# V in three column tiles with its third part behind the scores, one-bank turns of K and Q, and the attention weights turned in the forward pass

## The chip, the cores and the metric

The kernel runs on one core of a Trainium2 chip. The metric is the time of one execution on the device in microseconds (us), the median of several runs. The engines are PE (TensorE; PEld are its weight loads), DVE (VectorE), ACT (ScalarE), POOL (GpSimd) and SP (SyncE, which here only issues DMAs).

## The reference

The reference computes a block's output and the gradients of eleven of its inputs, all in bf16 (2048 tokens, width 512). The block is an adaLN-modulated recurrent memory attention followed by a gated GLU:

```python
def _A_ref(x, mem0, Wq, Wk, Wv, Wo, seg_len):        # seg_len 32, M = 8, H = 32 heads of 128
    mem = mem0
    for s in range(n_seg):                            # 64 segments, one after the other
        h = concat([mem, xs], axis=1)                 # 8 + 32 tokens
        q, k, v = h @ Wq, h @ Wk, h @ Wv              # per head
        p = softmax(where(mask, q k^T * scale, -1e9))
        o = (p v) @ Wo
        mem = o[:, :M]                                # the next segment's memory
        outs.append(o[:, M:])

def _fwd_reference(...):
    sa, ca, ga, sb, cb, gb = silu(c) @ w_mod
    x = x + ga * _A_ref(layernorm(x) * (1 + ca) + sa, ...)
    h = layernorm(x) * (1 + cb) + sb
    return x + gb * ((sigmoid(h @ w_gate) * (h @ w_up)) @ w_down)

out, vjp = jax.vjp(_fwd_reference, ...); grads = vjp(grad_out)
```

## The kernel before

`phase2` is the forward attention, `phase3` the GLU with its gradients and then the GLU's weight gradients, `phase4` the attention backwards, `phase5` the attention's weight gradients and the last layernorm. Instructions of the forward loop are pinned in the order in which the program writes them, on every engine and on SP (`self.pin(i0)`), so the order of the text is the order of work.

A segment has 40 tokens: 8 of memory and 32 of its own. The first 32 of them (memory and 24 tokens) depend on the segment before; the last 8 of four neighbouring segments do not, and are projected together for the group ("the tails", `b_pieces`, `proj_b`, 32 rows for the next group of four). `s4` is the place of a segment in its group.

`col_pass` is one pass of a projection: for each of four slices of the width, four matmuls of 512 columns that stand side by side in four column tiles of 32 rows. A pass covers 16 heads; tile j < 3 takes every third head of the first 24, tile 3 takes the heads 24 to 31. K, Q and V have two passes each. The result is copied to `RA[x]` (128 rows; `RAs` hold two of K and Q and one of V).

For K and Q the rows are turned by `turns` (eight transposes each into two half-filled PSUM banks) and copied into `XT[x]` by `to_heads`: "own" copies for tiles 0 to 2, "far" copies for tile 3. The first half of each goes by ACT, the second by DVE. For V, POOL copies 96 rows of `RA["v"]` into `Vst`, and `vshift` moves tile 3's heads to their rows by three small matmuls (into `sh_ps`) and one DVE copy. `v_tails` brings the tail rows of V into `Vst` by six DMAs on POOL's queue.

Then come the scores and their exponentials in three parts (`st_exp`), the denominators (`den`), the products with V (`pv`), the reciprocal and the scaling into `Ost` (part 1 on ACT, parts 0 and 2 on DVE), the turn of `Ost` into `OT` (`ott`), the product with Wo (`outproj`, into `at_ps`), its split in two bf16 halves (`split_pair`: `at_hi` on ACT, `at_lo` on DVE) and the fold (`sum_pair`, into `at_ft`). ACT copies `at_ft` into the memory columns of the next segment's `hT`, and with that the next segment's K can begin. Tail work fills PE ahead of the fold (`fill(s4, "f1")`) and behind it (`fill(s4, "f2")`): one pass of V, K and Q each at s4 = 0, 1, 2, and at s4 = 3 two chunks of 16 matmuls of the output projection of tails (`tail.chunk`). PSUM has five banks for all of these in turn (`psp`), and three for the scores.

SP's queue in a segment holds, in order: the stores of `VTr` and `Pst` of the segment before (the latter when POOL has scaled it), the row stores of K and Q (`rows_out`), two transposing DMAs (`VTr` from `Vst`, `Pst` from `ET`), and the stores of `Ost` (`OSR`) and `OT`. The tails' rows go in between.

Behind the GLU's pipeline, `phase3` computes the GLU's weight gradients (`wd_chunk` and the loop that follows it): 11 products of 512 columns and 32 of 448 columns, 16 matmuls each, whose rows are loaded by ACT's queue into a ring of two buffers. Between them `emit_setup` spreads 32 pieces from `p4_weights_setup_pieces`: each loads four heads of Wo, Wv, Wk or Wq (512 KB) into one of three staging slots, turns them by 16 transposes in four groups (into `wtp`), and DVE and ACT copy them to `WoT`, `WvT`, `WkT`, `WqT`, which `phase4` uses.

At the start, `load_heads` loads 24 heads of each of Wk, Wq, Wv in place and 8 to a staging place, from which three DVE copies put them in the order that tile 3 needs.

Of the kernel before, what the change touches and what calls it, by code (L numbers as in the profile page):

```python
# [40 lines left out]
class K:  # L41
# [43 lines left out]
    def alloc_dram(self):  # L85
# [26 lines left out]
        self.DHB = d("DHB", [NS // 4, 32, cfg.D], BF16)  # L112

# [323 lines left out]
    def phase2(self):  # L437
# [13 lines left out]
        with ExitStack() as ctx:  # L451
# [33 lines left out]
            RAs = [{x: ptiles(f"RA{i}" + x, 1, w=9 * 128)[0] for x in ("vkq", "kq")[i]} for i in range(2)]  # L485
            RAs[1]["v"] = RAs[0]["v"]
            RB = {x: ptiles("RB" + x, 1, w=9 * 128)[0] for x in "kq"}
            RBv = ptiles("RBv", 2, w=9 * 128)
# [17 lines left out]
            mem0 = pt.tile([M, D], BF16, name="mem0")  # L506
            with tc.tile_pool(name="p0", bufs=1) as p0:
# [14 lines left out]
                nc.sync.dma_start(mem0[:], io["A_mem0"].rearrange("o m d -> (o m) d"))  # L522
# [12 lines left out]
                place["v"] = self.load_heads(stage(2), Wv, io["A_Wv"])  # L535
# [70 lines left out]
            def b_pieces(t):  # L606

                bt = btails[t] = {}
                RBt = dict(RB, v=RBv[t % 2])

                def proj_b(x, hf):
                    hb = hxs[t][1]
                    pass_half(x, hf, lambda c: hb[:, c, :, :].rearrange("p s q -> p (s q)"), RBt[x], ("dve", "act")[hf])
                    if hf == 1 and x != "v":
                        rows_out(RBt[x], DR[x], t * nseg_t, nseg_t)

                def turn_b(x):
                    bt[x] = btp.tile([128, 8, 128], BF16, name="b_cols" + x)
                    tp = psp.tile([128, 8, 128], BF16, name="turn_ps", tag="p")
                    for i in range(8):  # L620
                        nc.tensor.transpose(tp[:, i, :], RBt[x][:, i * 128:(i + 1) * 128], self.ident[:, :])

                    def f():
                        for hf in range(2):
                            self.evac(("act", "dve")[hf], bt[x][:, 4 * hf:4 * hf + 4, :], tp[:, 4 * hf:4 * hf + 4, :])

                    evacs.append(f)

                P = lambda x, hf: (lambda: proj_b(x, hf))
                T_ = lambda x: (lambda: turn_b(x))  # L630
                d = {(s4, "f%d" % (hf + 1)): [P(x, hf)] for s4, x in enumerate("vkq") for hf in range(2)}
                d.update({(s4 + 1, "turn"): [T_(x)] for s4, x in enumerate("vkq") if x != "v"})
                return d
# [3 lines left out]
            def evac_turned():  # L637
                while evacs:
# [3 lines left out]
            firsts = {x: [f for k in ((s4, "f1"), (s4, "f2"), (s4 + 1, "turn")) for f in first.get(k, [])] + [evac_turned]  # L642
                      for s4, x in enumerate("vkq")}
            slots = {}

# [4 lines left out]
            norms = []  # L650
            mod_r = []
# [7 lines left out]
            tail = TailRows(self, sb2, psp, psp, 1, "ao", rows_b, 2, ptag="p")  # L659
# [14 lines left out]
            def v_tails(s):  # L674

                Vst, rb, o = Vsts[s % 2], RBv[(s // nseg_t) % 2], 8 * (s % nseg_t)
                for j in range(3):
                    nc.gpsimd.dma_start(Vst[96 + 8 * j:104 + 8 * j, 0:1024], rb[32 * j + o:32 * j + o + 8, 0:1024])
                    nc.gpsimd.dma_start(Vst[96 + 8 * j:104 + 8 * j, 1024:1408], rb[96 + o:104 + o, 384 * j:384 * j + 384])
# [9 lines left out]
            for s in range(NS):  # L689
# [11 lines left out]
                def proj(x, hf, eng):  # L701
                    pass_half(x, hf, lambda c: hT[:, c, :], RA[x], eng)
                    if hf == 1 and x != "v" and s < NS - 1:
# [6 lines left out]
                def turns():  # L710
                    tps = []
                    for x in "kq":
                        for hf in range(2):
                            tps.append((x, hf, ("act", "dve")[hf], turn_half(RA[x], hf)))
                            to_heads(tps[-1][2], XT[x], tps[-1][3][:], 4 * hf, 4, 32, 0, far=False)
                    for x, hf, eng, tp in tps:
                        to_heads(eng, XT[x], tp[:], 4 * hf, 4, 32, 0, own=False)
# [26 lines left out]

                def vshift():
                    sh = ps_f32("sh_ps")
                    shf = sh[:].rearrange("p g x -> p (g x)")
                    for hl in range(3):
                        nc.tensor.matmul(shf[32 * hl:32 * hl + 32, 0:384], lhsT=self.ident[96:128, 96:128],
                                         rhs=RA["v"][96:128, 384 * hl:384 * hl + 384], start=True, stop=True,  # L750
                                         tile_position=(96, 32 * hl))
                    nc.vector.tensor_copy(Vst[0:96, 1024:1408], shf[0:96, 0:384])
# [49 lines left out]
                if s == 0:  # L802
# [3 lines left out]
                    place["v"]()  # L806
                    load_wo(2)
                    for k in (1, 2, 3):
                        p1(1, k)
                    for f in firsts["v"]:  # L810
                        f()
                    v_tails(0)
                proj("v", 0, "dve")
                nc.gpsimd.tensor_copy(Vst[0:96, 0:512], RA["v"][0:96, 0:512])
                turns()
                proj("v", 1, "dve")
                nc.gpsimd.tensor_copy(Vst[0:96, 512:1024], RA["v"][0:96, 512:1024])
                if s == 0:
                    p1(1, 4)
                    p1(P1_AHEAD, 0)  # L820
                if s + 1 < NS:
                    v_tails(s + 1)
# [7 lines left out]
                vshift()  # L830
                st_exp(2)
                if s < NS - 1:
# [48 lines left out]
                self.pop_later()  # L881
                nc.sync.dma_start(self.OSR[s], gl3(Ost))
# [17 lines left out]
                fill(s4, "f2")  # L900
                if s4 == 3:
                    tail.chunk()
                tail.split()
# [53 lines left out]
    def phase3(self):  # L957
# [300 lines left out]
        with ExitStack() as ctx:  # L1258
            op_ = ctx.enter_context(tc.tile_pool(name="p3g_o", bufs=2, reuse_waits="tile"))
            psG = ctx.enter_context(tc.tile_pool(name="p3g_ps", bufs=4, space=PSUM, reuse_waits="tile"))  # L1260
            setup_pieces = self.p4_weights_setup_pieces(ctx)
# [80 lines left out]
    def p4_weights_setup_pieces(self, ctx):  # L1342
        nc, tc, cfg, io = self.nc, self.tc, self.cfg, self.io
        D, DC, H, E = cfg.D, cfg.DC, cfg.H, cfg.E
        HB = 4
        stg = ctx.enter_context(tc.tile_pool(name="p4stage", bufs=1, reuse_waits="tile"))
        sps = ctx.enter_context(tc.tile_pool(name="p4sps", bufs=2, space=PSUM, reuse_waits="tile"))
        pieces = []
        kk = [0]
        slots = [stg.tile([128, DC * HB * E], BF16, name=f"stage{i}") for i in range(2)]  # L1350
        slots = [t[:, :] for t in slots] + [self.flat(self.Wv, 2 * cfg.NT * 448, DC * HB * E)]
        np_ = [0]

        def slot(pat, **kw):
            np_[0] += 1
            return slots[np_[0] % 3].rearrange(pat, **kw)

        def qkv_piece(src_ap, dst, h0):
            def f():
                srcv = src_ap.rearrange("(c p) h e -> p c h e", p=128)  # L1360
                wn = slot("p (c h e) -> p c h e", c=DC, e=E)
                nc.sync.dma_start(wn, srcv[:, :, h0:h0 + HB, :])
                for hi in range(HB):
                    h = h0 + hi
                    tp = sps.tile([128, DC, 128], BF16, name="wtp")
                    for c in range(DC):
                        nc.tensor.transpose(tp[:, c, :], wn[:, c, hi, :], self.ident[:])
                    self.evac("dve" if kk[0] % 3 != 2 else "act", dst[:, h, :], tp[:, :, :].rearrange("p c d -> p (c d)"))
                    kk[0] += 1
            return f  # L1370

        def wo_piece(h0):
            def f():
                wov = io["A_Wo"].rearrange("h e d -> e h d")
                won = slot("p (h d) -> p h d", h=HB)
                nc.sync.dma_start(won, wov[:, h0:h0 + HB, :])
                for c in range(DC):
                    tp = sps.tile([128, HB, 128], BF16, name="wtp")
                    for i in range(HB):
                        nc.tensor.transpose(tp[:, i, :], won[:, i, c * 128:(c + 1) * 128], self.ident[:])  # L1380
                    self.evac("dve" if kk[0] % 3 != 2 else "act", self.WoT[:, c, h0 * E:(h0 + HB) * E],
                              tp[:, :, :].rearrange("p i e -> p (i e)"))
                    kk[0] += 1
            return f

        for h0 in range(0, H, HB):
            pieces.append(wo_piece(h0))
        for (src_ap, dst) in ((io["A_Wv"], self.WvT), (io["A_Wk"], self.WkT), (io["A_Wq"], self.WqT)):
            for h0 in range(0, H, HB):
                pieces.append(qkv_piece(src_ap, dst, h0))  # L1390
        return pieces

    def p4_weights_setup_transposes(self):
        with ExitStack() as ctx:
            for f in self.p4_weights_setup_pieces(ctx):
                f()

    def phase4(self):
# [3 lines left out]
        if not hasattr(self, "p4_ctx"):  # L1402
            self.p4_ctx = ExitStack()
            self.p4_weights_setup_begin()
            self.p4_weights_setup_transposes()
# [758 lines left out]
```

## Time and profile before

| | us |
|---|---|
| median of 3 runs | 3081.47 (3080.04 to 3082.02) |
| the profiled execution | 3080.64 |
| its span | 3078.9 |
| forward attention, first to last K pass | 18.9 to 977.4 |
| GLU weight gradients, until the attention backwards begins | 1346.0 to 1522.9 |
| mean granted clock of TensorE | 0.991 |

| stretch (us) | PE busy | DVE busy | ACT busy | POOL busy | DMA share |
|---|---|---|---|---|---|
| 100 to 500 | 395.84 | 239.62 | 211.69 | 278.73 | 0.80 |
| 500 to 1200 | 673.34 | 458.86 | 344.94 | 392.21 | 0.85 |

The profile is of one execution. A row of its order of time gives the start, the duration, the engine, the line, the operation, its output and inputs, the shape and the count; in square brackets stands the idle time of the engine ahead of it and what ended that. Matmuls overlap, so that what one adds to the path is the distance to the next start rather than its duration. The segments start about every 14.7 us.

### The profile page before, as it was taken

Reading aid. Unit: us, or ns where it says so; the run is one execution under the profiler, and the core shown is the slowest. Engines: PE = TensorE matmul, PEld = TensorE weight load, DVE = VectorE, ACT = ScalarE, POOL = GpSimd, SP = SyncE. Lnnn points to the kernel's source line nnn. Section 1 sums busy time; section 2 is a strip of 40 time slices with the busy share of each in tenths; the row PEclk is TensorE's granted clock in tenths of the full one; section 3 lists DMA queues with packets and bytes.
Section 4 is the critical chain, followed back from the end, with each engine's and each line's share of the span. In section 5 each row is a group of like instructions: output and inputs, shape, how many; then the busy total and the mean of one; then the engine's idle time right before and its main releaser. Section 6 shows DMA issues by size and latency. Waiting matters only on the chain.

```text
span 3078.9 us, 106050 instructions
## 1 busy us (share of the span) xinstructions
PE 2985.9 (97%) x43769; PEld 1821.5 (59%) x43845; DVE 1613.0 (52%) x3799; ACT 1254.4 (41%) x3056; POOL 1386.1 (45%) x2960
## 2 busy tenths in 40 slices
PE   6999999999999799989899999999999999999999
PEld 3666666666665444445577777777777754445455
DVE  4556656665655788742255555555555632322221
ACT  2555555555555433322155555555555520111011
POOL 3666767667766222211244444444444422333322
PEclk8999999999999899999999999999999999999999
DMA  8888788788778799997599999999999998666574
GB/s 300 217 215 204 204 209 217 203 214 212 206 202 255 199 229 231 225 282 254 176 232 246 244 247 246 245 248 244 248 243 245 253 278 278 201 194 221 188 236 149
DMA packets 845992, 703.54 MB, mean 229 GB/s; under 512 B 544354, under 2 KB 717954, under 8 KB 845124
## 3 DMA queue, kind: packets, MB, share of 16 engines
q1 hardware_dynamic: 714196, 486.69, 62.7%
q0 software_dynamic: 60656, 148.64, 15.1%
q10 hardware_dynamic: 70656, 61.41, 6.4%
q8 instruction: 345, 5.65, 0.8%
q14 instruction: 139, 1.14, 0.1%
HBM read 294.93 MB, written 276.35 MB: 186 GB/s over the span
## 4 chain that ended last, share of the span: by engine, by line
PE 45%; issue 3%; POOL 1%; DMA 1%; DVE 0%; ACT 0%; SPq 0%; POOLq 0%
PE gps L1954 9%; PE dh_ps L215 8%; PE g_ps L1616 6%; PE pass_ps L255 5%; PE gps5o L1968 5%; PE dhq_ps L223 4%; PE dh_tps L215 3%; PE dp_ps L1593 2%; PE tps L1526 2%; PE dp_ps L1601 1%; PE turn_ps L1480 1%; PE dh_ft L323 1%; POOL out_dram L1958 1%; DMA dhb<-DHA 0%; PE turn_ps L264 0%
## 5 line engine op out<-in xcount | busy, mean ns | idle before, releaser
L1954 PE MATMUL gps<-rows,hrows 128*128 128x512 bf16 (+2 forms) x2124 | 415.6, 355 | 1.9
L1954 PEld LDWEIGHTS <-hrows 128*128 128x128 bf16 x2160 | 211.3, 98 | 204.5
L255 PEld LDWEIGHTS <-hT 128*32 128x32 bf16 x6144 | 158.3, 97 | 168.5 <-DMA Wq<-in_A_Wq_dram 5.5
L1660 POOL COPY dOst<-RAd 96x512 bf16<-96x512 bf16 x128 | 75.5, 613 | 311.4 <-DVE RAd L63 311.2
L63 DVE CAST ot<-gps 128x512 bf16<-128x512 f32 (+3 forms) x76 | 48.1, 633 | 286.9 <-PE gps L1954 188.4
L1958 POOL DMA_DIRECT2D out_dram<-ot x108 | 81.5, 755 | 255.9 <-DVE ot L63 137.2
L61 ACT ACTIVATE ot<-gps 128x512 bf16<-128x512 f32 (+3 forms) x75 | 41.3, 551 | 352.3 <-PE gps L1954 230.7
L909 POOL TENSOR_TENSOR Pst<-Pst,rden 120x1408 bf16<-120x1408 bf16 x63 | 159.7, 2536 | 47.7 <-issue 21.4
L61 ACT ACTIVATE dVT<-g_ps 128x480 bf16<-128x480 f32 (+1 forms) x192 | 104.7, 545 | 95.5 <-PE g_ps L1616 95.1
L63 DVE CAST RA0v<-pass_ps 128x512 bf16<-128x512 f32 x128 | 88.5, 692 | 91.2 <-PE pass_ps L255 85.3
L255 PE MATMUL pass_ps<-Wv,hT 128*32 128x512 bf16 x2048 | 134.2, 382 | 0.0
L215 PE MATMUL dh_ps<-WvT,dVT 128*32 128x512 bf16 x2048 | 133.4, 380 | 0.3 <-DVE RBd L63 0.2
L255 PE MATMUL pass_ps<-Wq,hT 128*32 128x512 bf16 x2048 | 123.3, 383 | 5.3 <-DMA Wq<-in_A_Wq_dram 5.3
L1968 PE MATMUL gps5o<-WoT,rows 128*128 128x512 bf16 x580 | 127.7, 379 | 0.6
L223 PE MATMUL at_ps<-Wo,OT 128*32 128x256 bf16 x4096 | 124.6, 274 | 3.0 <-DMA Wo<-in_A_Wo_dram 3.0
L255 PE MATMUL pass_ps<-Wk,hT 128*32 128x512 bf16 x2048 | 121.6, 379 | 2.2 <-ACT hT L899 1.1
L255 PE MATMUL pass_ps<-WoT,dyT 128*32 128x256 bf16 (+1 forms) x3072 | 122.4, 308 | 0.9 <-ACT dyT L1734 0.9
L223 PE MATMUL dhq_ps<-WqT,dQT 128*32 128x256 bf16 x4096 | 122.9, 273 | 0.0
L215 PE MATMUL dh_ps<-WkT,dKT 128*32 128x512 bf16 x2048 | 122.3, 380 | 0.0
L223 PEld LDWEIGHTS <-dQT 128*32 128x32 bf16 x4096 | 109.6, 97 | 15.9
L1603 DVE SCALAR_TENSOR_TENSOR dS<-dp_ps,Pst_l 128x480 bf16<-128x480 f32 (+1 forms) x192 | 106.1, 608 | 19.2 <-PE dp_ps L1601 19.2
L223 PEld LDWEIGHTS <-OT 128*32 128x32 bf16 x4096 | 103.8, 97 | 18.6 <-issue 6.5
(421 smaller groups left out, 7034.9 us busy)
## 6 DMA issues: line engine op xcount, KB each, us to landing
OSR<-Ost SPq DMA_DIRECT2D x64, 352.0 KB
OT<-OT SPq DMA_DIRECT2D x64, 352.0 KB
VT<-VTr SPq DMA_DIRECT2D x64, 352.0 KB
PS<-Pst SPq DMA_DIRECT2D x64, 352.0 KB
OT_l<-OT SPq DMA_DIRECT2D x64, 352.0 KB
Pst_l<-PS SPq DMA_DIRECT2D x64, 352.0 KB
VT_l<-VT SPq DMA_DIRECT2D x64, 352.0 KB
DVR<-rows_x POOLq DMA_DIRECT2D x64, 352.0 KB, 6.2
```

What stands on the lines that cost most here:

```text
L61: return nc.scalar.activation(out, in_, AF.Copy)
L63: return nc.vector.tensor_copy(out, in_)
L215: self.nc.tensor.matmul(ps[32 * j:32 * j + 32, :], lhsT=lhsT, rhs=w, start=(n < 4), stop=(n >= total - 4), tile_position=(0, 32 * j))
L223: nc.tensor.matmul(ps[32 * j:32 * j + 32, :], lhsT=x[k], rhs=w[k][:, 256 * d:256 * d + 256], start=(n == 0), stop=(n == total - 1), tile_p ...
L255: self.nc.tensor.matmul(ps[32 * j:32 * j + 32, :], lhsT=lhs(c), rhs=rhs, start=(c == 0), stop=(c == DC - 1), tile_position=(0, 32 * j))
L909: nc.gpsimd.tensor_tensor(Pst[0:120, :, :], Pst[0:120, :, :], rden[:, :].unsqueeze(2).to_broadcast([120, G, 128]), op=ALU.mult)
L1603: nc.vector.scalar_tensor_tensor(out=part3(dS, pi)[:, :, 0:120], in0=ps[:, 0:n, 0:120], scalar=cfg.scale, in1=part3(Pst, pi)[:, :, 0:120], ...
L1616: nc.tensor.matmul(ps[:, j, 0:w], lhsT=lh[:, g * GW:(g + 1) * GW], rhs=rh[:, g * GW:g * GW + w], start=True, stop=True)
L1660: nc.gpsimd.tensor_copy(dOst[0:96, 512 * hf:512 * hf + 512], RAd[0:96, 512 * hf:512 * hf + 512])
L1954: nc.tensor.matmul(ps[:, 0:ng * E], lhsT=hrows[:, tp_, c * 128:(c + 1) * 128], rhs=rows[:, tp_, 0:ng * E], start=(tp_ == 0), stop=(tp_ == ...
L1958: nc.gpsimd.dma_start(outw[c * 128:(c + 1) * 128, h0:h0 + 3 * (ng - 1) + 1:3, :], ot[:, 0:ng * E].rearrange("p (h e) -> p h e", e=E))
L1968: nc.tensor.matmul(pss[gg][:], lhsT=src[0][:, src[1], gg * E:(gg + 1) * E], rhs=dyrows[:, tp_, :], start=(tp_ == order[0]), stop=(tp_ == o ...
```

## The change

V. Tile 3 no longer holds heads of V. `v_chunk` computes V in three parts of 4, 4 and 3 heads for each of the tiles 0 to 2, straight to the rows where `Vst` wants them; DVE copies each part to `Vst` (two copies for the third). In the fourth column tile it computes the tails of the next group. The first two parts stand where V's passes stood, the third behind the scores. `vshift`, POOL's copies and the reordering of Wv at the start go, and `v_tails` has three DMAs in place of six.

Turns. K is turned into one bank and copied by ACT alone, Q into another and copied by DVE alone.

Fold. The tails of K and Q are spread over the places ahead of the fold; the tail output projection is cut into 24 and 8 matmuls. Behind the fold stand eight transposes of attention weights (`weight_turns`), at s4 = 3 the chunk of 8; at s4 = 3 the weight turn stands behind the third part of V.

Weights. Each of the 64 segments turns one piece (two heads of Wk, Wv or Wq, or eight blocks of Wo), DVE copies it to `wt_rows` and SP stores it (256 KB) to a DRAM tensor `WT`. `p4_weights_setup_pieces` becomes sixteen loads of 1 MB from `WT`. The weight gradients get six PSUM banks in place of four.

```diff
+            VCH = ((0, 4), (4, 4), (8, 3))
+            def v_evac(eng, dst, ps, a, n):
+                m = n if a + n < G else n - 1
+                self.evac(eng, dst[0:96, a * E:(a + m) * E], ps[0:96, 0:m * E])
+                if m < n:
+                    self.evac(eng, dst[0:64, (a + m) * E:(a + n) * E], ps[0:64, m * E:n * E])
...
+            def v_chunk(s, k):
+                t, s4 = s // nseg_t, s % nseg_t
+                a, n = VCH[k]
+                tail_of = None
+                if t + 1 < NT:
+                    tail_of = (s4,) + VCH[k] if s4 < 3 and k < 2 else (k,) + VCH[2] if s4 == 3 else None
+                ps = psp.tile([128, 512], F32, name="pass_ps", tag="p")
+                hT = get_ht(s)
+                for c in range(DC):
+                    for j in range(3):
+                        v_mm(ps, j, c, hT[:, c, :], j, a, n)
+                    if tail_of:
+                        v_mm(ps, 3, c, hb_rows(t + 1)(c), *tail_of)
+                if k > 0:
+                    v_evac("dve", Vsts[s % 2], ps, a, n)
+                if tail_of:
...
+                    self.evac(("act", "dve", "dve")[k], RBv[(t + 1) % 2][32 * hl:32 * hl + 32, ta * E:(ta + tn) * E],
+                              ps[96:128, 0:tn * E])
+                if k == 0:
+                    v_evac("dve", Vsts[s % 2], ps, a, n)
...
+            def weight_turns():
+                while stores_wt:
+                    stores_wt.pop()()
+                x, h = wt_pieces.pop(0)
+                tp = psp.tile([128, 8, 128], BF16, name="wt_ps", tag="p")
+                for i in range(8):
...
+                    nc.tensor.transpose(tp[:, i, :], src, self.ident[:, :])
+                st = sb2.tile([128, 8, 128], BF16, name="wt_rows", bufs=1)
+                for i in range(2):
+                    self.evac("dve", st[:, 4 * i:4 * i + 4, :], tp[:, 4 * i:4 * i + 4, :])
...
+                return lambda: nc.sync.dma_start(dst, st[:].rearrange("p i d -> p (i d)"))
...
-            tail = TailRows(self, sb2, psp, psp, 1, "ao", rows_b, 2, ptag="p")
+            tail = TailRows(self, sb2, psp, psp, 1, "ao", rows_b, (24, 8), ptag="p")
...
-                d = {(s4, "f%d" % (hf + 1)): [P(x, hf)] for s4, x in enumerate("vkq") for hf in range(2)}
-                d.update({(s4 + 1, "turn"): [T_(x)] for s4, x in enumerate("vkq") if x != "v"})
-                return d
+                return {(0, "f1"): [P("k", 0, 4, "dve"), P("k", 4, 2, "act")], (1, "f1"): [P("k", 6, 2, "dve"), P("q", 0, 4, "act")],
+                        (2, "turn"): [T_("k")], (2, "f1"): [P("q", 4, 4, "dve")], (3, "turn"): [T_("q")]}
...
                 def turns():
-                    tps = []
-                    for x in "kq":
-                        for hf in range(2):
-                            tps.append((x, hf, ("act", "dve")[hf], turn_half(RA[x], hf)))
-                            to_heads(tps[-1][2], XT[x], tps[-1][3][:], 4 * hf, 4, 32, 0, far=False)
-                    for x, hf, eng, tp in tps:
-                        to_heads(eng, XT[x], tp[:], 4 * hf, 4, 32, 0, own=False)
+                    for x, eng in (("k", "act"), ("q", "dve")):
+                        tp = psp.tile([128, 8, 128], BF16, name="turn_ps", tag="p")
+                        for i in range(8):
+                            nc.tensor.transpose(tp[:, i, :], RA[x][:, i * 128:i * 128 + 128], self.ident[:, :])
+                        for hf in range(2):
+                            to_heads(eng, XT[x], tp[:, 4 * hf:4 * hf + 4, :], 4 * hf, 4, 32, 0, far=False)
+                        to_heads(eng, XT[x], tp[:], 0, 8, 32, 0, own=False)
...
                 st_exp(0)
                 st_exp(1)
-                vshift()
                 st_exp(2)
+                if s + 1 < NS:
+                    v_chunk(s, 2)
+                    v_tails(s + 1)
+                if s4 == 3:
+                    stores_wt.append(weight_turns())
...
+                while stores_wt:
+                    stores_wt.pop()()
                 nc.sync.dma_start(self.OSR[s], gl3(Ost))
...
-                fill(s4, "f2")
                 if s4 == 3:
                     tail.chunk()
+                else:
+                    stores_wt.append(weight_turns())
...
+        def load(x, dst, i):
             def f():
+                if x == "o":
+                    nc.sync.dma_start(dst[:, i // HB, :], self.WT[x][:, i // HB, :])
+                else:
+                    nc.sync.dma_start(dst[:, i:i + HB, :], self.WT[x][:, i:i + HB, :])
             return f
```

## The prediction

> **What bounds the kernel now.** I read the engine shares first, then the order of time on TensorE (PE) in one forward segment, then VectorE (DVE) in the same segment, then SyncE's queue (SP), then PE in the weight gradients behind the GLU.
>
> ```profile
> span 3078.9 us, 106050 instructions
> PE 2985.9 (97%) x43769; PEld 1821.5 (59%) x43845; DVE 1613.0 (52%) x3799; ACT 1254.4 (41%) x3056; POOL 1386.1 (45%) x2960
> ```
>
> PE is busy for 97% of the span. The order of time of PE in the segment that runs from 476.39 to 490.97 (the second of its group of four, s4 = 1):
>
> ```profile
> 481.81 1.05 PE L255 MATMUL pass_ps<-Wv,hT 128*32 128x512 bf16 x16
> 482.79 0.59 PE L724 MATMUL st_ps<-qT,kT 128*128 128x120 bf16 x8
> 483.31 0.74 PE L749 MATMUL sh_ps<-RA0v,ident 32*32 32x384 bf16 x3
> 483.99 0.33 PE L724 MATMUL st_ps<-qT,kT 128*128 128x120 bf16 x3
> ...
> 485.75 1.01 PE L742 MATMUL tps<-ident,Ost 120*128 120x120 bf16 x11
> ...
> 488.71 1.04 PE L255 MATMUL pass_ps<-Wk,hb 128*32 128x512 bf16 x16
> 489.68 0.27 PE L240 MATMUL at_ft<-foldsel,at_hi 128*128 128x32 bf16 x4
> ...
> 490.09 1.05 PE L255 MATMUL pass_ps<-Wk,hb 128*32 128x512 bf16 x16
> 490.97 1.90 PE L255 MATMUL pass_ps<-Wk,hT 128*32 128x512 bf16 x32
> ```
>
> Prices on PE are distances from start to start. A pass of 16 column-tiled matmuls of 512 columns costs 0.88 us when another such pass follows (490.09 to 490.97) and 0.97 when full-array work follows; so a round of four is 0.217 us and the change of tiling costs about 0.1. The three small matmuls that shift the last V heads cost 0.68 us. Nothing waits: the forward is a string of PE work, and segments of s4 = 0, 1, 2, 3 repeat at 14.83, 14.58, 14.69 and 14.90 us. DVE in the same segment:
>
> ```profile
> 482.98 0.69 DVE L63 CAST RA0v<-pass_ps 128x512 bf16<-128x512 f32 x1 [0.32 <-PE pass_ps L255]
> 484.09 0.55 DVE L752 CAST Vst<-sh_ps 96x384 bf16<-96x384 f32 x1 [0.42 <-PE sh_ps L749]
> 484.76 0.21 DVE L735 RECIPROCAL rden<-or_ps 120x8 f32<-120x8 f32 x1
> 485.00 0.69 DVE L771 TENSOR_TENSOR Ost<-or_ps,rden 120x512 bf16<-120x512 f32 x1
> 485.61 0.17 DVE L735 RECIPROCAL rden<-or_ps 120x3 f32<-120x3 f32 x1
> 485.81 0.56 DVE L771 TENSOR_TENSOR Ost<-or_ps,rden 120x384 bf16<-120x384 f32 x1
> ```
>
> From 484.09 on DVE has no gap, and PE's turn of Ost (485.75) starts just as the first Ost is written (485.00 + 0.69): here DVE has no slack to give. Last, SP and the weight gradients:
>
> ```profile
> 513.80 0.43 SPq L593 DMA_DIRECT2D QST<-RA1q  x1
> 516.44 1.62 SPq L839 DMA_TRANSPOSE Pst<-ET  x1
> ```
> ```profile
> 522.58 2.54 POOL L909 TENSOR_TENSOR Pst<-Pst,rden 120x1408 bf16<-120x1408 bf16 x1 [2.87 <-DMA Pst<-ET]
> ```
> ```profile
> 1352.59 0.71 PE L1380 MATMUL wtp<-ident,stage 128*128 128x128 bf16 x8 [1.65 <-DVE WoT L63]
> 1353.82 0.38 PE L1380 MATMUL wtp<-ident,Wv 128*128 128x128 bf16 x4
> 1362.75 1.03 PE L1380 MATMUL wtp<-ident,stage 128*128 128x128 bf16 x8 [3.89 <-DMA stage<-in_A_Wo_dram]
> ```
>
> A DMA issued at 516.44 lets POOL start only at 522.58: landing takes microseconds. The trace's semaphore records (sixteenth update after the issue) give, over the steady segments, medians of 3.1 to 3.3 us (2.4 to 4.6) for the Q row stores of s4 = 3 and 4.3 to 4.5 (2.9 to 5.2) for the Ost store that follows the two transposing DMAs.
>
> **The change, part by part.** Times are in us per group of four segments, of which there are 16.
>
> *GLU, removed.* 512 transposes go: four take 0.22 (1353.82 to 1354.04, the next PE row), so 128 x 0.22 = 28. Their waits go too: 1.65, 3.89 and, in later rows, 0.92, 1.08 and some 1.5 of small ones, 9 together. What stays is 11 x 16 x 0.217 + 32 x 16 x 0.189 = 135 of matmuls, against 177 now (1346.0 to 1522.9). Nothing paces the sixteen 1 MB loads any more once staging tiles are gone, so they press against the row loads, which already take 8 to 11 us to land. The chunk after the last of `wd_chunk` asks for rows 6.9 us after its buffer is freed; that is a wait of about 4, and I allow 4 more for the earlier rows. Gain 177 - 148 = 29; bounds 38 (no wait is added) and 20 (the loads cost 13 more).
>
> *V passes.* The shift (0.68) goes; V's third part comes in behind the scores: four rounds of 384/512 x 0.217 = 0.65, plus 0.1 for the tiling, 0.76. Its product for the next group's tails rides in the fourth column, so the two tail passes of V go from the fold. What ends late is DVE: the third part ends 0.25 after the shift did (0.17 of scores now come first, 0.08 is its own size), and is copied by two instructions instead of one (256 and 128 columns: 0.34 and 0.27, from 424 ns for 256 columns of at_lo and 553 for 384, spaced as DVE's rows are) before the reciprocal. Reciprocal, Ost and PE's turn of Ost move by about 0.25; at s4 = 0, 0.56 of modulation products covers a little. Sum for s4 = 0, 1, 2: +0.7 (0.4 to 1.0). POOL loses two copies and three DMA issues per segment, which nobody waited for.
>
> The Trainium skill, "TensorEngine Tiling (Array Packing)", PSUM Bottleneck, says that tiling speeds the matmuls but not the evacuation; by it the V edit moves work to the wrong engine. The rows here agree in kind: 96 partitions of 384 columns still take 553 ns.
>
> *Turns of K and Q.* One ACT chain and one DVE chain, 10 copies in place of 12. The far copies ended at 497.29 in the next segment with scores asking from 497.37; the new chains end within 0.3 of that, and the third score group is asked for 0.5 later. I cost it at nothing; without that cover, 0.3 per segment (+1.2).
>
> *Fold.* Passes now: 6 of 512 columns and two tail chunks, 4 x (0.97 + 0.88) = 7.40. Then: K and Q only, 1.40 + 1.40 + 0.97, and tails of 24 and 8 matmuls, 1.40 + 0.43; sum 5.60. Three weight turns of eight transposes (0.46, as K's eight from 480.81 to 481.27, and 0.08 of tiling) add 1.62. At s4 = 1 ACT copies a pass ahead of hT: +0.12. Sum -0.06 (-0.3 to +0.3). The turn just covers the 0.4 that hT takes.
>
> *The weight turn at s4 = 3.* It stands behind the third V part, ahead of reciprocal and Ost on DVE: 0.54 on PE, and on DVE a third tail copy (0.35) and two copies of 512 bf16 columns (424 ns each, as WoT's; 0.70 spaced). With the V shift, PE's turn of Ost moves by 1.3 (0.9 to 1.7) instead of 0.25.
>
> *The store's buffer.* `wt_rows` has one buffer: DVE's copy waits until the store before it has landed, and everything behind it on DVE waits too. At s4 = 3 that store is issued in the same segment, behind the Q row stores. These are issued 7.6 after the segment's start now; with the tail rows of Q out 1.3 earlier I put the store at 6.3, landing 3.3 later at 9.6. The third V part ends at 7.9; DVE copies it from 8.07 in 0.34 + 0.20 + 0.34 and wants the buffer at 8.95. Wait 0.65 at that, 0.5 taken since rows land early as often as late (0 if it lands early, 2.4 if SP stays where it is). PE waits for Ost at once. At the ends of s4 = 1 and 2 the store stands behind the transposing DMAs (issue 11.75 and 12.2, landing 4.25 and 4.5 later at 16.0 and 16.7). Q's second pass needs the bank of at_ft 3.14 after the fold (0.54 + 3 x 0.87), and DVE needs 1.3 for two copies and at_tb before that is free: PE can bear a landing 1.84 after the fold, at 16.4 and 15.9. Wait 0.8 in sum (0 to 2.2).
>
> The Trainium skill, "DMA: Bandwidth & Descriptors", gives a fixed 2.0 us plus bytes / 436e3 per us: for 256 KB an estimate of 2.6. By it the store of s4 = 3 lands at 8.9 and the 0.5 is gone, 8 us in all; the rows' 3.1 to 3.3 decide.
>
> Forward: 0.7 - 0.06 + 1.3 + 0.5 + 0.8 = 3.24, x 16 = +52 (17 if all are at their low ends, 122 at their high ends). *Start:* V loads by one DMA, three copies on DVE (1.5) go, 12 more matmuls (0.65) come and V waits for the second tile's turn; PE waits 2.95 at 59.25 for Wo anyway: 0 (-1 to +3). 16.8 MB of stores add 0.7 us of all DMA engines per segment, which leave gaps now (DMA share 0.80 to 0.85).
>
> Sum: +52 - 29 = +23. The profiled execution took 3080.64 (span 3078.9 and 1.7 around it), 0.8 under the median of 3081.47: forecast 3104.
>
> **Rivals.** *R1, faster:* the DVE order behind the scores costs PE nothing. Place: from the third V part to the turn of Ost. If reciprocal and Ost keep their place against PE and stores land in time, only PE's own sum is left, 4 x 0.08 + 0.54 - 0.06 = 0.8 per group, +13, while the GLU gives up to 38: 3056. It decides when the forward costs under 1.8 per group (29 / 16). For: DVE is 52% busy and PE has fillers at s4 = 0, 2, 3. Against: the gapless DVE rows from 484.09.
> *R2, slower still:* SP keeps its lateness at s4 = 3 and the GLU is short of DMA: waits of 2.4 and 2.2 (+53 over mine), gain 20: up to 3165, halfway 3135. For: 7.6 us issue of Q rows, landings up to 5.2. Against: the Q tail rows leave earlier.
> *R3, no change:* forward +29, as the GLU gives: 3081; the waits for stores absent, DVE's delay as summed.
>
> **How the numbers follow.** Forecast case (3088 to 3122) 0.46; R1 (3050 to 3075) 0.30; R2 (3122 to 3165) 0.14; R3 0.10. About 0.2% (6 us) is what a measurement can tell: faster 0.30, same 0.10, slower 0.60. The range 3062 to 3140 leaves out a third of R1 and half of R2; the forecast's own range is 3088 to 3122.
>
> **What would show it.** Right: at s4 = 3 DVE idle before the copy into wt_rows, ended by a DMA; s4 = 3 over 16 us, s4 = 1 near 15, s4 = 2 near its 14.7 or above; no wtp rows behind the GLU, which ends 25 to 33 us sooner after its pipeline. Wrong: segments of 14.6 to 14.8 throughout (R1), PE waits for Wv row loads of over 13 us behind the GLU (R2), or PE waits in K's and Q's turns, which I put at nothing.

## The result and the profile after

The changed kernel takes 3178.26 us (median of 4 runs, 3176.38 to 3186.64) against 3080.76 (3079.89 to 3082.02) for the kernel before on the same chip: ratio 1.0321, interval 1.0302 to 1.0341. It is slower by 97.5; the forecast was slower by 23. The profiled execution took 3179.95 (span 3178.1).

The engine shares of the changed kernel's page answer to the first lines of the prediction:

```profile
span 3178.1 us, 106343 instructions
PE 2995.9 (94%) x44158; PEld 1855.5 (58%) x44229; DVE 1645.1 (52%) x3916; ACT 1234.5 (39%) x2994; POOL 1216.2 (38%) x2640
```

PE is busy for 10 us more in a span that is 99 longer, so nearly all of the loss is waiting. Landmarks on PE (the first K pass of a segment, the first GLU product, the first product of the weight gradients, the first product of the attention backwards) cut the two profiled executions into pieces that can be subtracted:

| piece | before | after | difference |
|---|---|---|---|
| start, to the second segment | 63.64 | 61.48 | -2.2 |
| second to last segment | 912.23 | 1003.48 | +91.3 |
| last segment, to the GLU | 40.18 | 56.33 | +16.2 |
| GLU pipeline | 329.96 | 329.01 | -1.0 |
| GLU weight gradients, to the first product of the backward | 191.02 | 184.25 | -6.8 |
| the rest | 1541.85 | 1543.53 | +1.7 |

Segments of s4 = 0, 1, 2, 3 repeat at 14.97, 14.91, 14.50 and 20.5 us (medians; the last from 18.2 to 22.5), where they took 14.83, 14.58, 14.69 and 14.90. So the forward loses in one segment of four. First a segment of the other kind, s4 = 1, in the order of time on PE (start, duration, line, output and inputs, idle time ahead in brackets):

```profile
457.35 0.83 PE L651 MATMUL pass_ps<-Wv,hT 128*32 128x384 bf16 x12
...
459.81 1.01 PE L819 MATMUL tps<-ident,Ost 120*128 120x120 bf16 x11
...
464.39 0.61 PE L715 MATMUL wt_ps<-ident,Wv 128*128 128x128 bf16 x8
465.12 1.91 PE L256 MATMUL pass_ps<-Wk,hT 128*32 128x512 bf16 x32
```

V's third part (457.35) stands behind the scores, and the weight turn behind the fold (464.39) ends where the next K begins: the foreseen picture. The same view in the fourth segment, whose first K pass starts at 479.62:

```profile
492.82 0.48 PE L827 MATMUL or_ps<-Vst,ET 128*128 128x128 bf16 x3 [3.38 <-DVE rden L812]
493.09 0.27 PE L807 MATMUL or_ps<-ones,ET 128*128 128x1 bf16 x3
493.22 1.01 PE L621 MATMUL turn_ps<-ident,RBq 128*128 128x128 bf16 x8
494.03 0.61 PE L819 MATMUL tps<-ident,Ost 120*128 120x120 bf16 x4
```

PE stands still for 3.38 us, and eight transposes then take 0.81 from start to start (493.22 to 494.03) where they take 0.46 elsewhere. DVE in that stretch:

```profile
488.56 0.43 DVE L63 CAST RBv<-pass_ps 32x256 bf16<-32x256 f32 x1
491.90 0.76 DVE L63 COPY wt_rows<-wt_ps 128x512 bf16<-128x512 bf16 x2 [2.91 <-DMA WTv<-wt_rows]
492.57 0.20 DVE L812 RECIPROCAL rden<-or_ps 120x8 f32<-120x8 f32 x1
```

DVE waits 2.91 us for the store of the piece before, with the reciprocal behind it. SP's queue shows why the store is late; it is issued 7.98 after the segment's start:

```profile
479.98 2.12 SPq L597 DMA_DIRECT2D QST<-RBq  x3
482.14 1.83 SPq L600 DMA_DIRECT2D QST<-RBq  x3
...
487.10 0.45 SPq L593 DMA_DIRECT2D QST<-RA1q  x1
487.60 0.48 SPq L721 DMA_DIRECT2D WTv<-wt_rows  x1
```

The windows of PE ahead of the wait and behind it (length, busy time, granted clock, DMA share, GB/s):

```profile
480.00:489.00 9.00, 8.89 (x163) 1.00 0.88 316
492.80:495.70 2.90, 2.88 (x26) 0.51 1.18 300
```

After the wait the clock is 0.51 for 2.9 us. Over the fifteen such segments PE's idle time has a median of 3.38 (2.20 to 4.74), and the way from its end to the output projection takes 3.5 (2.26 in the kernel with the early store below). The trace's clock record drops to 0.5 at the end of fourteen of these waits; only at the shortest, 2.20, it does not, and the way behind that one takes 2.54. The Trainium skill, "TensorE: Matmul & The Clock Gate", Part 1, says that an idle window of about 3.4 us halves the clock and a busy one of that length restores it. The rows agree in size, though waits of 2.44 to 3.1 already did it here.

The last segment, in the order of time of SP and of DVE:

```profile
1074.60 6.71 SPq L1023 DMA_DIRECT2D Wv<-AOA  x4
...
1090.64 3.48 SPq L721 DMA_DIRECT2D WTo<-wt_rows  x2
```
```profile
1093.00 0.76 DVE L63 COPY wt_rows<-wt_ps 128x512 bf16<-128x512 bf16 x2 [20.26 <-DMA WTo<-wt_rows]
```

Here the store of the piece before stands behind the GLU's first loads and `late_rows`, and the same buffer holds DVE up for 20.26 us. Last, PE in the GLU's weight gradients:

```profile
1492.85 18.84 PE L1286 MATMUL gps<-Wk,Wv 128*128 128x512 bf16 x78 [21.67 <-DMA Wv<-HHROWS]
...
1522.15 8.13 PE L1371 MATMUL gps<-Wv,Wk 128*128 128x448 bf16 x31 [10.14 <-DMA Wv<-DGROWS]
```

The transposes are gone, and 31.8 us of waits for row loads stand in their place.

### The profile page after: what moved, and what is told of

It reads as the page before. It is cut to its first block, busy times and chain, and to the rows that moved or that the text cites. A ratio compares the mean times of both kernels' runs of the same rounds, so it can differ in the third digit from the quotient of the medians.

```text
span 3178.1 us, 106343 instructions
## 1 busy us (share of the span) xinstructions
PE 2995.9 (94%) x44158; PEld 1855.5 (58%) x44229; DVE 1645.1 (52%) x3916; ACT 1234.5 (39%) x2994; POOL 1216.2 (38%) x2640
## 5 line engine op out<-in xcount | busy, mean ns | idle before, releaser
L651 PE MATMUL pass_ps<-Wv,hT 128*32 128x512 bf16 (+2 forms) x2304 | 186.3, 357 | 0.0
L63 DVE CAST Vst<-pass_ps 96x512 bf16<-96x512 f32 (+2 forms) x256 | 126.6, 515 | 104.8 <-ACT RBv L61 95.1
L256 PEld LDWEIGHTS <-hT 128*32 128x32 bf16 x4096 | 109.9, 97 | 114.1 <-issue 6.3
L342 POOL DMA_DIRECT2D AOA<-at_rb x64 | 36.4, 568 | 308.6 <-DVE at_rb L338 308.6
L827 PE MATMUL or_ps<-Vst,ET 128*128 128x128 bf16 x704 | 67.9, 221 | 78.5 <-DVE rden L812 71.9
L651 PE MATMUL pass_ps<-Wv,hb 128*32 128x512 bf16 (+2 forms) x576 | 130.0, 366 | 0.0
L756 POOL DMA_DIRECT2D Vst<-RBv x192 | 100.3, 527 | 76.1 <-DVE RBv L63 47.3
```

The source lines that it names most:

```text
L63: return nc.vector.tensor_copy(out, in_)
L256: self.nc.tensor.matmul(ps[32 * j:32 * j + 32, :], lhsT=lhs(c), rhs=rhs, start=(c == 0), stop=(c == DC - 1), tile_position=(0, 32 * j))
L651: nc.tensor.matmul(ps[32 * j:32 * j + 32, 0:n * E], lhsT=lhsT, rhs=wc[:, 3 * a + hl:3 * (a + n - 1) + hl + 1:3, :], start=(c == 0), stop=( ...
L756: nc.gpsimd.dma_start(Vst[96 + 8 * j:104 + 8 * j, :], rb[32 * j + o:32 * j + o + 8, :])
```

## The experiments

Two causes were tried. Theory A: the wait for the one buffer of `wt_rows`, through the place of its store on SP, makes the fourth segments and the last one long. Theory C: the turned weights' loads, which nothing paces, hold up the row loads of the weight gradients. Ratios are to the kernel before on the same chip.

**Two buffers.** The memory for the second comes from writing the tail's split halves to `RB["k"]`.

```diff
-                st = sb2.tile([128, 8, 128], BF16, name="wt_rows", bufs=1)
+                st = sb2.tile([128, 8, 128], BF16, name="wt_rows", bufs=2)
-            tail = TailRows(self, sb2, psp, psp, 1, "ao", rows_b, (24, 8), ptag="p")
+            tail = TailRows(self, sb2, psp, psp, 1, "ao", rows_b, (24, 8), home=RB["k"], ptag="p")
```

> wt_rows gets two buffers; the 2 KB for it come from letting the tail split write its halves into RBk, which is free then. Theory A (the copy into wt_rows waits for the store before it): segments of s4 = 3 fall from 20.4 us to about 16.2 (14.9 + the 1.3 that the turn and its copies take on PE and DVE), the last segment loses its wait of 20, and the kernel comes to about 3098. Theory B (what costs is where the turn stands and what it does to PE's clock, not the wait for the store): s4 = 3 stays above 19 and the kernel above 3160.

Measured: 3098.88, ratio 1.0057 (1.0042 to 1.0072). Periods 14.97, 14.91, 14.49, 16.19; last segment 42.6; the weight gradients 183.2 with waits of 30.9. Theory B asked for a fourth period above 19 and falls. Four fifths of the loss are the one buffer.

**Loads on GpSimd's queue**, alone and with the two buffers.

```diff
-                    nc.sync.dma_start(dst[:, i:i + HB, :], self.WT[x][:, i:i + HB, :])
+                    nc.gpsimd.dma_start(dst[:, i:i + HB, :], self.WT[x][:, i:i + HB, :])
```

> The sixteen 1 MB loads behind the GLU are issued by POOL, between the output stores for which POOL waits, instead of all at once by SP; nothing else differs from the changed kernel. Theory C (unpaced loads starve the row loads): the waits of 21.7 and 10.1 us behind the GLU fall under 5 in all, and the kernel comes to about 3150. Rival C2 (the stage moves the same bytes in less time and is bound by DMA whatever the order): waits of 20 or more remain, spread over the products, and the kernel stays within 10 of 3178.

> Two buffers and POOL's loads together. Theories A and C: the savings add, 3178 - 80 - 28 = about 3070, 10 under the kernel before. With B or C2 in the place of one of them it stays above 3095.

Measured: 3177.30 alone (1.0309, 1.0277 to 1.0341) and 3097.08 with two buffers (1.0047, 1.0032 to 1.0061), no gain in either. The waits for row loads only moved: 12.2 + 14.9 on lines 1286 and 1371 in the first, 15.0 + 15.2 in the second. Taken by themselves both results are those of the rival C2. The queue did change the pace: SP issued the sixteen loads from 6 to 49 us after the stage's start, GpSimd from 6 to 81 and 84, nearly each behind the store of a product. Twice the time was not enough.

**Weights turned behind the GLU again**, with V's three parts, the one-bank turns and the new fold kept; `weight_turns` goes and `p4_weights_setup_pieces` is the one of before.

```diff
-                if s4 == 3:
-                    stores_wt.append(weight_turns())
...
-                else:
-                    stores_wt.append(weight_turns())
```

> The attention weights are turned behind the GLU as before the change; V's three tiles, the one-bank turns and the new fold stay, and nothing but the small chunk at s4 = 3 stands behind the fold. Theory A and C: the forward loses 2.2 us of turns per group against the changed kernel but PE then waits some 0.4 for hT three times per group, so a group takes 59.0 to 59.6 (59.0 before) and the kernel 3080 to 3092. Rival (V's third part on DVE is the main cost of the forward): over 60.5 per group and above 3105.

Measured: 3099.72, 1.0059 (1.0043 to 1.0074), and 59.94 per group: between the two branches, a miss of both. Periods 14.97, 14.90, 14.48, 15.52. The first three equal those with the weight turns: behind the fold a turn costs nothing, since PE waits for `hT` there anyway. V, turns of K and Q and fold cost 0.93 per group (from the groups between the fifth and the sixty-first segment: 839.20 - 826.24 over 14), and the turn at s4 = 3 another 0.67 (848.56 with two buffers).

**The fourth turn behind the fold, one buffer.**

```diff
-                if s4 == 3:
-                    stores_wt.append(weight_turns())
...
                     tail.chunk()
-                else:
-                    stores_wt.append(weight_turns())
+                stores_wt.append(weight_turns())
```

> The whole change with its one buffer of rows, but in every fourth segment (s4 = 3) the weight turn stands behind the fold, as in the other three, and not between st_exp(2) and den(0). If the wait for the store before is what makes that segment long (theory A: 2.9 us of DVE on the store, 0.8 more on PE in its front, 1.0 of a lower granted clock behind it), the copy now comes some 4 us after the store is issued and waits about as little as at the ends of the other segments: periods 15.0, 14.9, 14.5 and 16.1 to 16.8, the last segment still 50 or more (its store still sits behind the late loads), median 3104 to 3116. If the turn itself is dear at s4 = 3 whatever its place (rival: PE and DVE are full there), the fourth period stays above 18 and the median above 3135.

Measured: 3112.82, 1.0093 (1.0079 to 1.0106); fourth period 16.18; last segment 47.8, a little under the 50 expected. Place and buffer make the wait together: the turn in its old place with two buffers, or one buffer with the turn behind the fold, gives the same period.

**The turns of K and Q alone**, put into the kernel before.

```diff
-                    tps = []
-                    for x in "kq":
+                    for x, eng in (("k", "act"), ("q", "dve")):
+                        tp = psp.tile([128, 8, 128], BF16, name="turn_ps", tag="p")
```

> The kernel before, with the turns of K and Q in one bank each and nothing else of the change. The prediction put these at nothing (PE's second turn hides ACT's copies), 0 +- 0.2 per cent: 3075 to 3087. Without that cover it had +1.2 per group of four segments: 3100.

Measured: 3085.19, 1.0007 (0.9998 to 1.0016), no difference; the periods are 14.83, 14.58, 14.69 and 14.91.

**The store issued at once**, one buffer, everything else as in the change.

```diff
                 else:
-                    stores_wt.append(weight_turns())
+                    weight_turns()()
```

> The change with its one buffer and its places, but the store of each piece turned behind a fold is issued at once, ahead of the next segment's work on SP's queue, and not held back to the next flush. If the fourth segment is long because the store stands behind the stores of K's and Q's rows (theory A: issued 8.0 us after the segment's start, landed 4.2 later), it now lands before 5 us and the copy in the middle finds its buffer free: periods 15.0, 14.9, 14.5 and 16.2, the last segment 43, median 3096 to 3106 with one buffer as with two. If the transfer itself is slow, or SP's wait for DVE's copies holds up the stores behind it (rival), the fourth period stays above 17.5 or the others grow by 0.3 or more: 3120 or more.

Measured: 3101.59, 1.0062 (1.0047 to 1.0077): within the interval of two buffers, from one line. Periods 14.98, 14.91, 14.50, 16.19; last segment 42.3. SP, DVE and PE of a fourth segment (start 456.80), each in its order of time:

```profile
460.68 0.38 SPq L721 DMA_DIRECT2D WTv<-wt_rows  x1
```
```profile
465.90 0.76 DVE L63 COPY wt_rows<-wt_ps 128x512 bf16<-128x512 bf16 x2
466.57 0.20 DVE L812 RECIPROCAL rden<-or_ps 120x8 f32<-120x8 f32 x1
```
```profile
466.82 0.33 PE L827 MATMUL or_ps<-Vst,ET 128*128 128x128 bf16 x3 [0.50 <-DVE rden L812]
```

The store goes 3.88 after the segment's start and lands at 6.00, 2.12 later, by the semaphore records; the copy waits for nothing, PE for 0.50 instead of 3.38, and its clock is 1.00 behind that. This settles theory A: the wait comes from the store's place on SP's queue. From the earlier place it is both issued sooner and landed in half the time.

**Loads spread in the text**, two buffers, on GpSimd's queue.

```diff
+                if fc in (6, 10):
+                    setup_pieces.pop(0)()
...
+                        if c % 2 == 0 and setup_pieces:
+                            setup_pieces.pop(0)()
```

> The change with two buffers of rows (3099 when it ran alone), and the sixteen loads of turned weights in the weight-gradient stage handed out by time: two among the eleven products of w_down, fourteen among the 32 products of w_gate and w_up, each behind the store of a product on GpSimd's queue. If the 31 us for which PE waits there for row loads come from the burst of unpaced loads (theory C), the waits fall to under 12 us and the median to 3076 to 3084. If they come from the amount of data (rival: 16 MB more beside 8 MB of rows in the same time, whenever they are issued), the waits stay at 25 or more and the median at 3093 or more.

Measured: 3100.54, 1.0049 (1.0035 to 1.0063), a miss of both branches: waits 14.2 + 3.0, stage 171.1 in the profiled execution, which was the fastest of the four (3094.76), and no gain in the median. The edit did not do what its text says: order is not pinned in this stage, and the planner issued twelve of the sixteen loads between 1380.7 and 1431.9.

**48 turns, Wo behind the GLU**, two buffers, the twelve loads spread in the same way.

```diff
-            wt_pieces = [(x, h) for x in "kvq" for h in range(0, H, 2)] + [("o", (c, h)) for c in range(DC) for h in range(0, H, 8)]
+            wt_pieces = [(x, h) for x in "kvq" for h in range(0, H, 2)]
...
-                if s4 == 3:
-                    stores_wt.append(weight_turns())
```

> The change with two buffers of rows, no weight turn in the fourth segments: 48 turns (K, V, Q) behind the folds of the other three, where they were free; Wo is turned in the weight-gradient stage as before, and the twelve loads of K, V, Q are spread over it. Forward as with the weights turned in the GLU (periods 15.0, 14.9, 14.5, 15.6: +14 against the kernel before); the stage 193 minus three quarters of 32 pieces' 1.2 us, 165, if the spread loads cost no wait (theory): median 3068 to 3076, faster than the kernel before by 0.2 to 0.4 per cent. If the loads still hold the row loads up by 15 us or more (rival): 3084 or more.

Measured: 3100.82, 1.0051 (1.0037 to 1.0064). The forward came out as expected (period 15.53 at s4 = 3), the stage did not: 190.8, row waits of 12.5 + 3.9 and another 6.8 on DVE's copies into `WoT`. The rival held, but here too the order in the text was not the order on the queue. What does the stage move? Windows of the stage in the changed kernel (length; busy time and count of PE, PEld, DVE, ACT, POOL; clock, DMA share, GB/s):

```profile
1450.00:1522.00 72.00, 39.83 (x173) 17.49 (x176) 4.15 (x6) 3.24 (x6) 8.37 (x19) 0.82 1.03 382
1522.00:1552.00 30.00, 29.85 (x147) 15.00 (x148) 2.50 (x4) 2.43 (x5) 4.34 (x8) 0.93 0.45 145
```

For 72 us the DMA engines are full and PE is busy for 40; then PE is full and they are half idle. Whether the order or the bytes were at fault, a pinned order had to show.

**Loads in half pieces, pinned**, two buffers.

```diff
+                if fc < 11:
+                    setup_pieces.pop(0)()
...
+                        if c < 3 and setup_pieces:
+                            setup_pieces.pop(0)()
...
+            self.pin(g0, [ET.Pool])
```

> The change with two buffers of rows, and the loads of the turned weights in half pieces of 512 KB: eight among the first eight products of w_down, one each, and 24 among the 32 products of w_gate and w_up, three for every four products; this time GpSimd's queue is pinned in the order of the text, so that each load stands behind the store of a product (in the run before the planner moved the loads ahead of those stores, and twelve of sixteen were issued in 50 us). By the windows of the change with two buffers the first 72 us of the stage moved data all the time (share 1.03, 382 GB/s), the 100 us behind them half of the time. If that uneven order is the cause of the waits (theory C), they fall from 31 us to under 12 and the median to 3074 to 3084. If PE waits for rows by 20 us or more in the stage all the same (rival: the bytes themselves), 3090 or more.

Measured: 3073.66, 0.9974 (0.9963 to 0.9985). The stage takes 156.8. PE's groups there (busy, mean ns, idle before and its releaser):

```profile
L1373 PE MATMUL gps<-Wv,Wk 128*128 128x448 bf16 x512 | 98.4, 356 | 4.6 <-DMA Wv<-DGROWS 4.6
L1286 PE MATMUL gps<-Wk,Wv 128*128 128x512 bf16 x133 | 29.5, 379 | 1.4 <-DMA Wv<-HHROWS 1.2
```

The waits fall from 31 to 5.8 with the same bytes, so the bytes are not the limit: theory C in a sharper form, when each load is issued. The loads now leave from 6 to 141 us after the stage's start, and the row loads land in 8.5 to 11.8. Smaller pieces, longer spacing and the pin came together here; no run separates them.

**48 turns, pinned.** The kernel of 48 turns with its loads in half pieces and the same pin.

> The forward with 48 turns behind the folds of s4 = 0, 1 and 2 and none in the fourth segments; Wo turned in the weight-gradient stage among the first products, and the loads of V, K and Q in half pieces, three for every four products of w_gate and w_up, on GpSimd's queue pinned in the order of the text. Forward +14 against the kernel before, as measured twice; the stage 191 less 28 for 24 turned pieces less, plus 0 to 8 of waits: 163 to 171 by theory C, median 3069 to 3079, the one version that could beat the kernel before. Rival (bytes): stage over 180, 3088 or more.

Measured: 3069.99, 0.9958 (0.9942 to 0.9975); stage 161.3, row waits under 1. What remains of the forward's loss is V's new layout and the fold, and its largest piece is at s4 = 3 (15.53 against 14.90). DVE there, then PE:

```profile
522.75 0.43 DVE L63 CAST RBv<-pass_ps 32x256 bf16<-32x256 f32 x1
523.21 0.21 DVE L812 RECIPROCAL rden<-or_ps 120x8 f32<-120x8 f32 x1
```
```profile
523.48 0.33 PE L827 MATMUL or_ps<-Vst,ET 128*128 128x128 bf16 x3 [0.47 <-DVE rden L812]
```

PE waits for the reciprocal behind the copy of the tails, while ACT has nothing to do.

**That copy on ACT**, in the kernel of 48 pinned turns.

```diff
-                    self.evac(("act", "dve", "dve")[k], RBv[(t + 1) % 2][32 * hl:32 * hl + 32, ta * E:(ta + tn) * E],
+                    self.evac(("act", "dve", "act")[k], RBv[(t + 1) % 2][32 * hl:32 * hl + 32, ta * E:(ta + tn) * E],
```

> The 48-turn version of the run before (3070, ratio 0.9958), with one copy moved: the tails that V's third part computes for the next group in every fourth segment go to their rows by ACT instead of DVE. In that version PE waits 0.47 us in those segments for the reciprocal, which stands on DVE behind that copy (0.43 us), while ACT is idle for 1.21 us. If DVE's chain behind V's third part is what V's new layout costs there (the prediction's V term), the fourth period falls from 15.53 to 15.10 and the median by 16 x 0.43 = 7, to 3063 (ratio 0.9937, 0.992 to 0.995). If ACT's copy delays Ost by as much (rival), the period stays at 15.5 or above and the median at 3070 or more.

Measured: 3062.58, 0.9938 (0.9926 to 0.9951), fourth period 15.13. It is faster than both kernels, by 18.5 us (0.6 per cent) against the one before. Its interval overlaps that of the run before; the period, 15.53 to 15.13, shows the gain. ACT in a fourth segment:

```profile
457.48 0.38 ACT L61 ACTIVATE RBv<-pass_ps 32x256 bf16<-32x256 f32 x1 [0.41 <-PE or_ps L827]
457.88 1.14 ACT L836 ACTIVATE Ost<-or_ps,rden 120x128 bf16<-120x128 f32 x4
```

ACT takes the copy in a gap and goes on to Ost without one.

## Why the prediction was right in direction and wrong in size

*V, turns, fold.* Predicted +0.64 for s4 = 0, 1, 2 (0.7 - 0.06); measured +0.28 (44.38 against 44.10). Its mechanism, DVE's gapless chain from V's third part to the turn of Ost, is confirmed at s4 = 3, where moving one copy off DVE gave back 0.40; at s4 = 0, 1, 2 no run separates V from the fold. The turns of K and Q cost nothing, as worked out, and the weight turns behind the fold cost nothing either.

*The turn at s4 = 3.* The segment was to lose 1.3 by it and V together; without the wait for the store it loses 1.29 (16.19 - 14.90). The split held too: 0.62 is V with its third tail copy (0.25 + 0.35 in the prediction), 0.67 the turn (0.70).

*The store's buffer*: the first failed step. The mechanism was right; the term was mis-sized. The text put the wait at s4 = 3 at 0.5 and its upper bound at 2.4; the loss is 4.5 per group (911.86 - 848.56 over 14).
- "I put the store at 6.3" was the wrong step, twice. In the kernel before, 7.6 is when the last Q row store itself is issued; it leaves SP at 8.07 (medians of fifteen segments), and the new store stands behind it, not in its place. And the tail rows of Q left SP 0.5 earlier (4.13 after the segment's start, against 4.63), not 1.3. In the segment shown their six stores hold SP until 484.0, and the store goes at 7.98. That adds 1.7.
- It lands 4.18 after its issue, not 3.3, behind the four row stores. Issued early, behind six smaller stores of tail rows, it takes 2.12. The Trainium skill, "DMA: Bandwidth & Descriptors", Anatomy of one DMA, gave an estimate of 2.6, from a fit to DMAs issued by GpSimd; it is near the median of the early stores (2.7) and too low for the late ones (3.7).
- DVE asks for the buffer at 9.37, not 8.95, so the wait is 0.65 + 1.7 + 0.9 - 0.4 = 2.9, as the profile has it.
- Missing from the sum: the slow clock behind the wait, 1.0 here. And the Q pass is longer by 0.3 (2.20 for 1.90), because the store at the end of s4 = 2 lands 2.5 after the fold, past the 1.84 that PE was to bear. That wait was in the prediction; its price of 0.8 was too high, since only four of fifteen Q passes were longer at all.

So 2.9 + 1.0 + 0.3 makes the 4.2 that this segment loses (20.37 - 16.19). Over the fifteen the means are 3.0, 1.2 and 0.1, nearly all of the 4.5. The rival "slower still" named this lateness of SP and a GLU short of DMA, and was given 0.14; even its end of 3165 lacks the clock and the last segment.

*The last segment* (+16.2) was no term at all. The prediction followed the store through SP's queue in a steady segment only; in segment 63 the queue holds four broadcasts, the GLU's loads and `late_rows` ahead of it. Two buffers or the early store give back 14 of the 16.

*GLU*: the second failed step. A gain of 29 was predicted with 8 us of row waits; the stage gained 6.8 with 31.8. "Nothing paces the sixteen 1 MB loads" was seen, but its price was set at two waits of 4: row loads that had taken 8 to 11 us to land were thought to stay near that, and five of them took 15 to 32 with 16.8 MB of loads queued beside them. The sign given for R2, a row wait of over 13 us, came (21.67). With the loads spread the gain is 34 (191.0 - 156.8), within the bounds of 20 to 38 (37 by the prediction's own terms, 28 + 9).

In sum, the profiled execution misses 76 (99 - 23): 39 between the second and the last segment, all of it in the fourth segments, 16 in the last one, 22 in the GLU's weight gradients, and -1 to -2 in the start, the GLU pipeline and the rest.

## What to carry to other kernels

Where a single buffer is emptied by a DMA, follow that DMA through its queue in the busiest segment and in the last one, and ask who stands ahead of it: issuing the store as soon as its data exist did here what a second buffer does. Work that is taken off an engine can take its pace off the transfers beside it, so give them a new pace that the scheduler can't move. Price a PE wait of some 3 us with the slow stretch behind it, 1.2 us here.

## What the runs showed of the hardware

- At the end of the fourteen waits of 2.44 to 4.74 us the granted clock fell to 0.5 for 3.4 us (6.8 at two of them), and at the one of 2.20 it did not; behind the 20 us of the last segment the output projection took 3.4 us where it takes 1.76 (start to start).
- A 256 KB store landed in 2.12 us behind six small stores (264 KB) and in 4.18 behind four row stores (528 KB); over the fifth to the sixtieth segment the medians were 2.7 with the early issue and 3.7 with the late one.
- In the GLU's weight gradients the DMA engines were full for 72 us at 382 GB/s, sixteen loads (16.8 MB) among the rest, and PE waited 31.8 us for rows. Issued by GpSimd over 75 us instead of 43 the loads left 27 to 30 us of waits; in half pieces over 135 us they left 5.8.
